# Earlier and later places for pieces of a hand-written schedule: spectral mixing, then routed experts, on one core

## The chip, the cores and the metric

One core of one Trainium2 chip runs the whole kernel in one launch. The metric is device time in microseconds: the median of three timed runs. A profile is one further execution under the hardware profiler, with a time of its own.

## What is computed

```python
X = np.fft.rfft(x, axis=1)                 # x: (8, 2496, 256), fp32
F = (filt_r + 1j * filt_i)[None, :, :]
y = np.fft.irfft(X * F, n=x.shape[1], axis=1)
x = y.reshape(19968, 256)
expert_idx = token_ids * 2654435761 % 8
for e in range(8):
    mask = expert_idx == e
    h = np.maximum(x[mask] @ w1[e], 0.0)   # w1: (8, 256, 1024)
    out[mask] = h @ w2[e]                  # w2: (8, 1024, 256)
```

A sequence of 2496 = 39 x 64 rows is transformed, filtered and transformed back; then every row goes through the one of eight two-layer networks that its token number picks.

## The kernel before, in words

**Mixing.** Each of the eight batches goes through three stages. Stage 1 takes the products of length 39 (`stage1`, six units, products `pa`, recorded at L267 and L261 with their copies on ScalarE); its result is written to a DRAM tile `d1` (L297) and read back in another layout (`load2`, L303). Stage 2 has ten blocks: `forward` (products `pb`, L312, and four VectorE operations: y at L318, two z at L322, the sum at L323) and `back` (products `pc`, L335, whose copies go through the DRAM tile `d2`). Stage 3 (`load4` reads at L406, `stage3` makes the products `pd`, again L267 and L261) puts rows into tiles `o`, and GpSimd scatters each of them (L433, an indirect DMA) into the array `xs`, at a place that belongs to the row's expert. In the first two batches parts are done on the chip in another form: `turn2` (transposes `pt`, L367), `back_c` (products `pc`, L378, copied at L380) and `turn4` (transposes `pu`, L394).

**Experts.** `xs` is cut into 85 tiles of 256 rows, ordered in five stages so that the tiles of a stage need the first 2, 3, 4, 6 or all 8 batches. Step i works on tile i: `up` (eight groups of products in banks a, b, c, L886, with sums of weights that GpSimd prepares at L876, a copy of bank a on ScalarE at L897, VectorE additions at L893 and relus on ScalarE at L890) and `down` (L921). The rows of a tile are asked for by `load`: four DMA issues of `xg` and one of `no` (L843), from tile 2 on out of ScalarE's queue. `ask(i)` loads tile i+2, if it has not been loaded; inside `down`, `spot` asks one tile further ahead when that tile belongs to the same stage. So the requests of an ordinary tile go out in `down`, and those of tile 2 and of the first tile of each later stage in `up`, at `ask(i)`.

**The order.** A manual schedule: what is written first stands first on its engine's queue. The list `head` holds pairs of a due number and a piece; the numbers only sort. Everything in `head` stands ahead of step 0: the table loads, the routing (`count`, `route`, `tile_experts`, `experts` on VectorE, `later` and `places` on GpSimd), the first two batches whole, stage 1 of the third and most of the fourth. `chain(k)` at 22+3k issues `turn2(k+1)`, `back_c(k-2)` and `forward(k)` of the first batch. The list `main` holds what is mixed into the steps: `part1`, `part2` and `part3` give stage 1, 2 and 3 of a batch numbers in steps, `within` squeezes them, and `run_until(t)` issues all with a number below t at fixed points: i+.6 ahead of `down`, i+.7, .8 and .9 inside it, i+1 after it.

**Buffers.** The products of all mixing stages share four PSUM buffers (`fps`); `y` and `z` share three SBUF buffers (`ppool`); the input tiles `x` of a batch share two (`xpool`). A piece that takes a buffer waits for the last reader of the piece that held it.

`warm(n)` multiplies the identity by itself n times into bank a; nobody reads the result.

Of the kernel before, what the change touches and what calls it, by code (L numbers as in the profile page):

```python
# [36 lines left out]
NU = (HN + XG) // XG  # L37
# [88 lines left out]
def kernel(  # L126
# [314 lines left out]
    first, second = batches[:2]  # L441
# [255 lines left out]
    def pads(k):  # L697
        blank = ppool.tile([P, 2 * C], I32, name=f"blank_{k}", tag="p")[:, 0:W]
        nc.vector.memset(blank[:, 0:C], 0)
        nc.vector.memset(blank[:, C:], N)  # L700
        for q in (2 * k, 2 * k + 1):
            scatter(blank.bitcast(F32), at_i[:, q:q + 1], "xs_pad")
# [19 lines left out]
    def spaced(t0, t1, n):  # L722
        return [t0 + (t1 - t0) * u / n for u in range(n)]

    def within(todo, share=.5):

        return [(t // 1 + .5 + t % 1 * share, piece) for t, piece in todo if t is not None]

    def part1(b, at, loads):
        bt = batches[b]  # L730
        return within([(at[u], lambda u=u: bt.stage1(u)) for u in range(NU)] +
                      [(loads[v], lambda v=v: bt.load1(v)) for v in range(NV)])

    def part2(b, at, loads, lag):
        bt = batches[b]
        return (within([(at[u], lambda u=u: bt.forward(u)) for u in range(NS // 2)], .3) +
                within([(at[u] + lag, lambda u=u: bt.back(u)) for u in range(NS // 2)] +
                       [(loads[g], lambda g=g: bt.load2(g)) for g in range(NS // SG)]))

    def part3(b, at, loads):  # L740
        bt = batches[b]
        return within([(at[u], lambda u=u: bt.stage3(u)) for u in range(NU)] +
                      [(loads[v], lambda v=v: bt.load4(v)) for v in range(NV)])
# [6 lines left out]
    def chain(k):  # L750

        for step, j in ((Batch.turn2, k + 1), (Batch.back_c, k - 2), (Batch.forward, k)):
            if 0 <= j < N_2:
                step(first, j)

    def warm(n):

        ps = banks["a"].tile([P, 4, P], F32, name="warm", tag="a")
        for k in range(n):
            nc.tensor.matmul(out=ps[:, k % 4, :], lhsT=ident[:], rhs=ident[:], start=True, stop=True)  # L760

    third = batches[2]
    head = [(0, lambda: warm(14))]
# [7 lines left out]
    head += [(t, lambda k=k: way_back(k)) for k, t in enumerate((21.91, 31.2))]  # L771
    head += [(21.95, lambda: first.turn2(0))]
    head += [(22 + 3 * k, lambda k=k: chain(k)) for k in range(N_2 + 2)]
    head += [(t, lambda u=u: second.stage1(u)) for u, t in enumerate((28.5, 31.5, 37.5, 40.5, 46.5, 47))]
    head += [(50 + .1 * g, lambda g=g: second.load2(g)) for g in range(4)]
    head += [(67, lambda: second.load2(4))]
    head += [(t, lambda u=u: first.room(u)) for u, t in enumerate((50, 53.5, 56.5, 61, 75.5, 80))]
    at = (56, 57.8, 63, 69, 75, 79.5)
# [5 lines left out]
    head += [(t, lambda k=k: weights(k // 2, k % 2)) for k, t in enumerate((90, 90.1, 90.2, 90.3))]  # L784
    head += [(90.2 + 4.6 * u - 1.5 * (u > 0), lambda u=u: [second.turn4(u), second.room(u)]) for u in range(NU)]
    head += [(91.8 + 4.6 * u, lambda u=u: second.stage3(u)) for u in range(NU)]
    head += [(93.3 + 4.6 * u + 4 * (u > 3), lambda u=u: third.stage1(u)) for u in range(NU)]
    head += [(100, blanks)]
    fourth = batches[3]
    head += [(t, lambda v=v: fourth.load1(v)) for v, t in enumerate((110.5, 110.6))]  # L790
    head += [(123.5, lambda: begin()), (123.6, lambda: [load(i) for i in range(2)])]
    head += [(124, lambda: [nc.sync.dma_start(out=dram, in_=chip) for dram, chip in put_off[2]])]
    head += [(125 + .1 * g, lambda g=g: third.load2(g)) for g in range(4)]
    head += [(126, lambda: [nc.sync.dma_start(out=dram, in_=chip) for dram, chip in put_off[3]])]
    head += [(123 + .1 * u, lambda u=u: fourth.stage1(u)) for u in range(4)]
    todo = [(t - 200, piece) for t, piece in head]
    todo += [(t, lambda k=k: pads(k)) for k, t in enumerate((10.9, 11.6, 11.9, 16.9, 17.6, 17.95, 22.9))]

# [8 lines left out]
        return out  # L807

    todo += part2(2, spaced(1, 3.5, N_2), [None] * 4 + [1.5], .6)
    todo += part3(2, spaced(4.6, 7.5, NU), [4.0, 4.1, 4.8]) + part1(3, [None] * 4 + [1.5, 2], [None, None, .5])  # L810
    todo += part2(3, spaced(6.4, 10, N_2), [5.2, 5.4, 5.6, 6.5, 7.5], .6)
    todo += part3(3, spaced(12, 16, NU), [11.2, 11.4, 12.5])
    todo += batch(4, (7.5, 11), (12.4, 16.4), (18.3, 22.3)) + batch(5, (13, 17), (18.4, 21.6), (23.2, 26.8))
# [1 line left out]
    for e in range(E):  # L815
        t = 34.3 + 1.5 * e
# [10 lines left out]
    def begin():  # L827
        nonlocal gath, work, outs, nums, tpool
        rctx.close()
        tpool, nums, gath = [pool(ctx, f"tp{k}", 1) for k in range(2)], pool(ctx, "nums", 8), pool(ctx, "gath", 2)  # L830
        outs, work = pool(ctx, "outs", 2), pool(ctx, "work", 1)
        weight_sums(0, nc.vector)

    def load(i):

        g = gath.tile([P, TB // 32, C // 4], F32, name=f"xg_{i}", tag="xg")
        no = nums.tile([P, 2], I32, name=f"no_{i}", tag="no")
        rows = xs[tiles[i] * TB:(tiles[i] + 1) * TB, :]
        moves = [(g[32 * q:32 * q + 32, :, :], rows[:, 64 * q:64 * q + 64].rearrange("(a t) c -> t a c", t=32))
                 for q in range(4)]  # L840
        moves.append((no[:].bitcast(F32), rows[:, C:C + 1].rearrange("(h p) c -> p (h c)", p=P)))
        for k, (to, src) in enumerate(moves):
            ld = (nc.sync if i < 2 and (i or k < 3) else nc.scalar).dma_start(out=to, in_=src)  # L843
            for b in range(STAGES[stage_of[i]], B):
                tc.declare_no_dep(ld.ins, group=f"xs_{b}", reason="the tiles of a stage hold tokens of its batches alone")
            if stage_of[i] < G - 1:
                tc.declare_no_dep(ld.ins, group="xs_pad", reason="places without a token lie in the last stage alone")
            tc.add_to_no_dep_group("xs_read", ld.ins)
        xg[i], to_rows[i] = g, no
# [26 lines left out]
            eng.tensor_tensor(t[k][:], p, q, op=OP.subtract)  # L876
        sums[i] = t

    def up(i, ht, between=lambda: None):
        w1, x, st, t = ws[i][0], parts[i], parts[i]["sums"], sums[i]  # L880
        ps = {k: banks[k].tile([P, 4, P], F32, name=f"up_{i}_{k}", tag=k) for k in "abc"}
        h11, h12, h21, h22 = [ht[:, h, 4 * f:4 * f + 4, :] for h in range(2) for f in range(2)]

        def product(bank, w, xx, first, fs=range(4)):
            for f in fs:
                nc.tensor.matmul(out=ps[bank][:, f, :], lhsT=w[:, f * P:(f + 1) * P], rhs=xx,  # L886
                                 start=first and f == 0, stop=True, skip_group_check=True)

        def relu(out, in_):
            nc.scalar.activation(out=out, in_=in_, func=AF.Relu)  # L890

        def plus(out, bank, other):
            nc.vector.tensor_tensor(out, ps[bank][:], other, op=OP.add)  # L893

        h = F // 2
        product("a", w1[:, 0, 0:h], x[0, 0], True)
        nc.scalar.copy(out=h21, in_=ps["a"][:])  # L897
        between()
        product("b", t[1], st[:, 1, :], True)
        plus(h12, "b", h21)  # L900
        product("c", t[0], st[:, 0, :], True)
        plus(h22, "c", h21)
        product("a", w1[:, 1, 0:h], x[0, 1], False, (0, 1))
        product("b", t[2], st[:, 2, :], False)
        plus(h22, "b", h22)
        relu(h22, h22)
        product("a", w1[:, 1, 0:h], x[0, 1], False, (2, 3))
        relu(h11, ps["a"][:])
        product("c", w1[:, 1, h:], st[:, 3, :], False)
        plus(h12, "c", h12)  # L910
        relu(h12, h12)
        product("b", t[3], x[1, 1], False)
        plus(h21, "b", h21)
        relu(h21, h21)
# [112 lines left out]
    def ask(i, sooner=False):  # L1027

        j = asked[0]
        if j <= i + 2 or (sooner and j == i + 3 < NT and stage_of[j] == stage_of[j - 1]):  # L1030
            if j < NT:
                load(j)
                asked[0] += 1
# [7 lines left out]
    def run_until(t):  # L1041
        while main and main[0][0] < t:
            main.pop(0)[1]()

    def late_step(i):
        ht = work.tile([P, 2, FP, P], F32, name=f"ht_{i}", tag="ht")
        store(i - 1, (1,))
        if i + 1 < NSURE:
            weight_sums(i + 1)
        store(i - 1, (0,))  # L1050
        both(i, ht)

    def step(i):
        if i >= WS:
            late_step(i)
            return
        ht = work.tile([P, 2, FP, P], F32, name=f"ht_{i}", tag="ht")
        if i + 1 < NSURE:
            weight_sums(i + 1)
        if i > 0:  # L1060
            store(i - 1)
        up(i, ht, lambda: ask(i))
        weights(i + 2, 0)
        if i + 1 < NSURE:
            token_parts(i + 1)
            token_sums(i + 1)
        run_until(i + .6)
        down(i, ht, lambda k: spot(i, k))
        weights(i + 2, 1)
        run_until(i + 1)  # L1070
# [59 lines left out]
```

## Time and profile before

| | us |
|---|---|
| median of 3 timed runs | 1466.7 (1465.14 to 1467.44) |
| the profiled execution: time, span | 1423.94, 1422.2 |
| mean granted TensorE clock in it | 0.991 |
| TensorE busy | 1372.1 |
| first up product (step 0 begins) | 141.38 |
| first scatter of the second batch | 106.50 |

How to read the profile: a line of the timeline has the start, the busy time, the engine, the line of the code, the operation, its output and inputs, and in brackets the idle time of that engine before it and what ended that. PE is TensorE, DVE VectorE, ACT ScalarE, POOL GpSimd, SP SyncE; a q behind the engine's name (ACTq, SPq) means its queue issuing a DMA. A line of the stretches has, for each engine, busy time and instructions, and at the end the granted TensorE clock as a share of full speed, the DMA engines' busy share and the GB/s that they moved.

### The profile page before, as it was taken

The numbers are of one execution on the slowest core, as the hardware profiler recorded it, in microseconds if no ns is written. First come the engines' busy times: TensorE is split into PE (matmuls) and PEld (weight loads), VectorE is DVE, ScalarE is ACT, GpSimd is POOL, SyncE is SP. The second block draws the span as 40 slices with busy tenths as digits, with TensorE's granted clock in tenths as the row PEclk, the third lists the DMA queues.
The fourth block names the chain that finished last, engine by engine and source line by source line (L and its number), as shares of the span: only waits on it lengthen the run. The fifth ranks groups of instructions, "written<-read, shape, count | busy, mean of one in ns | idle before, by whom it ended". The sixth has DMA issues, their size and how long they took to land.

```text
span 1422.2 us, 26307 instructions
## 1 busy us (share of the span) xinstructions
PE 1372.1 (96%) x9398; PEld 1272.3 (89%) x9398; DVE 888.2 (62%) x1630; ACT 417.2 (29%) x760; POOL 828.3 (58%) x735
## 2 busy tenths in 40 slices
PE   8988999999999999999999999999999999999997
PEld 7776888988888988889999899999999999999997
DVE  7673475575556566445766377656767776777775
ACT  4544122223232223232223222222222222222222
POOL 6157143844665565578533587788845566555563
PEclk9999899999999999999999999999999999999999
DMA  8786765858987698888754775887742526161611
GB/s 230 204 275 172 223 206 121 274 187 246 272 259 223 182 289 268 251 265 272 242 167 128 221 256 173 231 242 236 253 139 67 192 57 203 46 217 40 219 46 35
DMA packets 244650, 278.34 MB, mean 196 GB/s; under 512 B 125171, under 2 KB 213862, under 8 KB 235092
## 3 DMA queue, kind: packets, MB, share of 16 engines
q1 hardware_dynamic: 98020, 182.34, 40.7%
q10 hardware_dynamic: 126688, 50.07, 14.4%
q0 software_dynamic: 19808, 44.20, 8.8%
q8 instruction: 77, 1.26, 0.4%
q14 instruction: 57, 0.47, 0.1%
HBM read 293.65 MB, written 86.15 MB: 267 GB/s over the span
## 4 chain that ended last, share of the span: by engine, by line
PE 85%; DMA 7%; DVE 5%; issue 1%; ACT 1%; SPq 1%; ACTq 0%; POOL 0%; POOLq 0%; DVEq 0%
PE dps L921 20%; PE up_b L886 9%; PE up_a L886 6%; PE up_c L886 5%; PE pd L267 5%; PE pb L312 4%; PE dnc L948 4%; PE dnb L948 4%; PE upc L943 4%; PE dna L948 4%; PE upa L943 4%; PE pa L267 4%; PE pc L335 3%; PE upe L943 2%; PE upb L943 2%; PE upg L943 2%
## 5 line engine op out<-in xcount | busy, mean ns | idle before, releaser
L921 PE MATMUL dps<-wts,ht 128*128 128x256 f32 x1600 | 370.2, 382 | 4.9 <-ACT ht L890 4.9
L921 PEld LDWEIGHTS dps<-wts,ht 128*128 128x128 f32 x1600 | 304.3, 191 | 49.1 <-ACT ht L890 6.1
L1013 POOL DMA_INDIRECT out_dram<-osb,no x158 | 165.2, 1045 | 223.5 <-DVE osb L955 137.2
L433 POOL DMA_INDIRECT xs<-o,sidx x176 | 177.7, 1009 | 169.6 <-ACT o L269 94.0
L876 POOL TENSOR_TENSOR tw<-wts 128x512 f32<-128x512 f32 x158 | 204.3, 1293 | 110.9 <-DMA wts<-in_moe_w_dram 98.8
L876 POOL TENSOR_TENSOR tw<-wts,tw 128x512 f32<-128x512 f32 x158 | 206.1, 1304 | 6.2
L893 DVE TENSOR_TENSOR ht<-up_b,ht 128x512 f32<-128x512 f32 x150 | 103.7, 691 | 117.9 <-PE up_b L886 91.1
L890 ACT ACTIVATE ht<-ht 128x512 f32<-128x512 f32 x150 | 94.3, 630 | 189.0 <-DVE ht L893 169.0
L322 DVE TENSOR_TENSOR z<-pb,filt 64x512 f32<-64x512 f32 x160 | 110.2, 689 | 30.0 <-PE pc L335 28.0
L926 DVE COPY osb<-dps 128x512 f32<-128x512 f32 x50 | 34.5, 691 | 148.1 <-PE dps L921 147.8
L886 PE MATMUL up_a<-xt,wts 128*128 128x128 f32 x800 | 115.5, 277 | 11.0 <-ACT ht L897 6.3
L886 PEld LDWEIGHTS up_a<-xt,wts 128*128 128x128 f32 x800 | 105.9, 193 | 14.8 <-ACT ht L897 7.1
L886 PE MATMUL up_b<-st,tw 128*128 128x128 f32 x800 | 107.5, 278 | 3.6 <-DVE ht L893 2.2
L886 PEld LDWEIGHTS up_b<-st,tw 128*128 128x128 f32 x800 | 98.1, 193 | 5.7 <-issue 5.1
L893 DVE TENSOR_TENSOR ht<-up_c,ht 128x512 f32<-128x512 f32 x100 | 69.0, 690 | 38.0 <-PE up_c L886 33.2
L952 ACT ACTIVATE ht<-ht 128x512 f32<-128x512 f32 x90 | 56.6, 630 | 121.5 <-DVE ht L955 72.7
L267 PE MATMUL pd<-t,wi_t 120*117 120x256 f32 x320 | 77.5, 385 | 3.1 <-DMA t<-d 2.2
L318 DVE TENSOR_TENSOR y<-pb,filt 128x512 f32<-128x512 f32 x80 | 55.1, 689 | 40.5 <-PE pb L312 38.2
L323 DVE TENSOR_TENSOR y<-y,z 128x512 f32<-128x512 f32 x80 | 74.4, 930 | 2.7
L269 ACT COPY o<-pd 117x512 f32<-117x512 f32 x80 | 44.9, 585 | 101.6 <-PE pd L267 51.6
L897 ACT COPY ht<-up_a 128x512 f32<-128x512 f32 x50 | 29.4, 587 | 150.2 <-PE up_a L886 109.2
L312 PE MATMUL pb<-low,d_t 128*128 128x256 f32 x280 | 72.3, 381 | 0.6 <-DVE z L322 0.6
(215 smaller groups left out, 2422.5 us busy)
## 6 DMA issues: line engine op xcount, KB each, us to landing
wts<-in_moe_w_dram SPq DMA_DIRECT2D x162, 1024.0 KB
xg<-xs ACTq DMA_DIRECT2D x321, 64.0 KB
low<-d SPq DMA_DIRECT2D x70, 256.0 KB
d_t<-t2s SPq DMA_DIRECT2D x15, 1024.0 KB
e_t<-t2s SPq DMA_DIRECT2D x15, 1024.0 KB
x<-in_x_dram SPq DMA_DIRECT2D x39, 312.0 KB
t<-d SPq DMA_DIRECT2D x12, 960.0 KB
raw<-in_moe_w_dram SPq DMA_DIRECT2D x8, 1024.0 KB
```

The lines of the kernel that those rows point to most:

```text
L267: nc.tensor.matmul(out=ps[0:cols * H, k, :], lhsT=w[:], rhs=src[:, 2 * i + k, :], start=True, stop=True)
L312: nc.tensor.matmul(out=ps[:, i, :], lhsT=d_t[:, s, :], rhs=rhs, start=True, stop=True)
L322: nc.vector.tensor_tensor(out=z[b], in0=ps[a], in1=f_t[1][64 * hi:64 * hi + 64, s1:s1 + 2, :], op=OP.mult)
L433: st = nc.gpsimd.indirect_dma_start(out=xs[:], out_offset=bass.IndirectOffsetOnAxis(ap=index, axis=0), in_=rows, in_offset=None, bounds_ch ...
L876: eng.tensor_tensor(t[k][:], p, q, op=OP.subtract)
L886: nc.tensor.matmul(out=ps[bank][:, f, :], lhsT=w[:, f * P:(f + 1) * P], rhs=xx, start=first and f == 0, stop=True, skip_group_check=True)
L890: nc.scalar.activation(out=out, in_=in_, func=AF.Relu)
L893: nc.vector.tensor_tensor(out, ps[bank][:], other, op=OP.add)
L921: nc.tensor.matmul(out=ps[:, h, :], lhsT=ht[:, h, fp, :], rhs=w2[:, fp, :], start=(fp == 0), stop=(fp == FP - 1))
L943: nc.tensor.matmul(out=ps[:, f, :], lhsT=w[:, f * P:(f + 1) * P], rhs=xx, start=first and f == 0, stop=True, skip_group_check=True)
L948: nc.tensor.matmul(out=ps[:, 0, :], lhsT=a[:, f, :], rhs=b[:, f, :], start=first and f == 0, stop=True, skip_group_check=True)
L1013: st = nc.gpsimd.indirect_dma_start(out=out[:], out_offset=bass.IndirectOffsetOnAxis(ap=to_rows[i][:, h:h + 1], axis=0), in_=o[:, h, :], i ...
```

## The change

- Stage 1 of the second batch: units 0 and 1 one place of the chain later, units 4 and 5 after the forward products of block 9, around the back products of block 8. Its reads (`load2`) are numbered behind the last unit.
- Stage 1 of the third batch: units 0 and 1 ahead of the last two back products of the second batch's stage 2, units 2 and 3 where 0 and 1 were, units 4 and 5 at the end as before.
- The first two loads of the fourth batch's input are numbered 95 and 99.5 instead of 110.5 and 110.6.
- 14 idle products (`warm`) behind the fourth batch's stage 1, ahead of step 0.
- Stage 3 of the third batch about half an issuing point later. By the fixed points: unit 0 goes from inside `down` of step 4 to behind it, units 1 to 4 one point on, unit 5 stays.
- `ask(i)` goes from behind the copy of bank a to behind the whole of `up`, so behind the relus on ScalarE's queue. The late steps (from 50 on, `both`) are not changed.

```diff
-    head += [(t, lambda u=u: second.stage1(u)) for u, t in enumerate((28.5, 31.5, 37.5, 40.5, 46.5, 47))]
-    head += [(50 + .1 * g, lambda g=g: second.load2(g)) for g in range(4)]
+    head += [(t, lambda u=u: second.stage1(u)) for u, t in enumerate((31.5, 34.5, 37.5, 40.5, 49.5, 52.5))]
+    head += [(53 + .1 * g, lambda g=g: second.load2(g)) for g in range(4)]
...
-    head += [(93.3 + 4.6 * u + 4 * (u > 3), lambda u=u: third.stage1(u)) for u in range(NU)]
+    head += [(t, lambda u=u: third.stage1(u)) for u, t in enumerate((87, 89.9, 93.3, 97.9, 114.9, 115))]
...
-    head += [(t, lambda v=v: fourth.load1(v)) for v, t in enumerate((110.5, 110.6))]
+    head += [(t, lambda v=v: fourth.load1(v)) for v, t in enumerate((95, 99.5))]
...
+    head += [(123.55, lambda: warm(14))]
...
-    todo += part3(2, spaced(4.6, 7.5, NU), [4.0, 4.1, 4.8]) + part1(3, [None] * 4 + [1.5, 2], [None, None, .5])
+    todo += part3(2, spaced(4.85, 7.6, NU), [4.0, 4.1, 4.8]) + part1(3, [None] * 4 + [1.5, 2], [None, None, .5])
...
-    def up(i, ht, between=lambda: None):
+    def up(i, ht):
...
         product("a", w1[:, 0, 0:h], x[0, 0], True)
         nc.scalar.copy(out=h21, in_=ps["a"][:])
-        between()
         product("b", t[1], st[:, 1, :], True)
...
-        up(i, ht, lambda: ask(i))
+        up(i, ht)
+        ask(i)
         weights(i + 2, 0)
```

## The prediction

> **What bounds the kernel now.** I read the page's busy shares first, then the chain of waits, then TensorE's timeline for its gaps, and from each gap the timeline of the engine it waits for.
>
> ```profile
> PE 1372.1 (96%) x9398; PEld 1272.3 (89%) x9398; DVE 888.2 (62%) x1630; ACT 417.2 (29%) x760; POOL 828.3 (58%) x735
> PE 85%; DMA 7%; DVE 5%; issue 1%; ACT 1%; SPq 1%; ACTq 0%; POOL 0%; POOLq 0%; DVEq 0%
> ```
>
> TensorE is the bound: 96% busy, 85% of the chain. No matmul is removed, so only its gaps and its clock can change. Those that the edits touch:
>
> ```profile
> 29.64 1.96 PE L267 MATMUL pa<-wts,wf_t 117*120 117x256 f32 x8 [1.18 <-DMA wts<-in_x_dram]
> 32.87 1.13 PE L378 MATMUL pc<-e_t,y 128*128 128x128 f32 x8 [0.69 <-DVE z L322]
> 60.62 1.62 PE L378 MATMUL pc<-e_t,y 128*128 128x128 f32 x8 [2.11 <-DVE o L412]
> 69.04 1.03 PE L312 MATMUL pb<-low,d_t 128*128 128x256 f32 x4
> 141.38 2.08 PE L886 MATMUL up_a<-xt,wts 128*128 128x128 f32 x8 [4.66 <-DVE xt L854]
> 152.56 8.86 PE L921 MATMUL dps<-wts,ht 128*128 128x256 f32 x32 [2.27 <-ACT ht L890]
> 240.44 1.99 PE L267 MATMUL pd<-t,wi_t 120*117 120x256 f32 x8 [2.20 <-DMA t<-d]
> 501.64 3.54 PE L921 MATMUL dps<-wts,ht 128*128 128x256 f32 x8 [2.61 <-ACT ht L890]
> ```
>
> Columns: start, busy time, operation, the gap before it and who ended it. The first down products of step 0 (152.56) and of step 18 (501.64) wait for relus on ScalarE, whose timeline says why:
>
> ```profile
> 143.71 5.49 ACTq L843 DMA_DIRECT2D xg<-xs  x4
> 150.93 0.41 ACTq L843 DMA_DIRECT2D no<-xs  x1
> 151.39 0.63 ACT L890 ACTIVATE ht<-ht 128x512 f32<-128x512 f32 x1 [7.31 <-DMA xg<-xs]
> 494.37 4.51 ACTq L843 DMA_DIRECT2D xg<-xs  x4
> 500.47 0.63 ACT L890 ACTIVATE ht<-ht 128x512 f32<-128x512 f32 x1 [6.12 <-DVE xt L854]
> ```
>
> Issuing a tile's row requests held ScalarE 7.6 us (143.71 to 151.34) and 6.1 us, with the relus behind. The clock by stretch (one before the last figures):
>
> ```profile
> 33.00:38.00 5.00, 5.00 (x33) 4.62 (x34) 4.82 (x9) 2.84 (x5) 4.40 (x6) 1.00 0.96 282
> 140.00:147.00 7.00, 5.62 (x29) 5.62 (x30) 3.31 (x7) 0.59 (x1) 2.17 (x2) 0.54 0.84 192
> 498.00:505.00 7.00, 4.39 (x18) 3.54 (x17) 3.87 (x7) 2.15 (x4) 5.41 (x5) 0.76 1.06 292
> ```
>
> The clock fell to half after the gaps of 4.66, 2.61 and 2.27 us, not after 2.20. Lastly the queues that matter:
>
> ```profile
> 33.77 1.50 DVE L664 TENSOR_TENSOR past<-rt,last 128x40 f32<-128x40 f32 x1
> 36.78 1.39 DVE L322 TENSOR_TENSOR z<-pb,filt 64x512 f32<-64x512 f32 x2
> 60.35 13.44 SPq L303 DMA_DIRECT2D low<-d  x10
> 106.50 0.98 POOL L433 DMA_INDIRECT xs<-o,sidx  x1 [9.26 <-ACT o L269]
> 134.74 0.89 POOL L433 DMA_INDIRECT xs<-o,sidx  x1 [0.30 <-issue]
> ```
>
> **What the Trainium skill says.** "TensorE: Matmul & The Clock Gate", Part 1: the clock is halved after an idle window of about 3.4 us, returns after a busy one, and the windows run freely. The trace agrees in kind: gaps from 2.3 us up can halve it, for 3.0 to 6 us. "DMA: Bandwidth & Descriptors", Two DMAs through the same engine are not ordered: a DMA that reads what another wrote must wait for that one's semaphore. So the second batch's rows go out and back in full: last write issued at 56.7, reads at 60.35. "Perfetto Trace Analysis", Tensor Engine Instruction: ScalarE, VectorE and GpSimd are strict FIFO, as the relus behind the requests show.
>
> **Part by part**, against the profiled execution of 1423.94 us (span 1422.2 and 1.7 around it). The median of the timed runs is 42.8 us higher; I carry the difference over unscaled.
>
> *Second batch's stage 1 later.* The unit stood at 29.64 (1.73 us of TensorE by the pitch of its neighbours, two ScalarE copies; SP's writes follow the copies). Without it pc 1 needs y 1 alone (28.54+2.05=30.59) and starts at 30.74, pb 3 at 31.6, pe at 32.9, done 33.5. Then comes the moved unit, and in the changed program its PSUM buffer is the one that pb 3 held: it waits for z 3. VectorE reaches z 3 behind the tile_experts chain (L664 at 33.77 to L670 at 36.06) and ends it at 38.17. So TensorE stands idle from 33.5 to 38.3, 4.8 us, where it was wholly busy. After 4.66 us the clock fell; I expect it here too, some 4.2 us at half speed, 2.1 us lost. Counting on at the pitches of this stretch (pa 1.73, pt .58, pc .89, pb .87, VectorE 2.85 a block): pa 38.3 to 41.8, pb 4 at 43.5 (38.35 before), pb 7 at 56.0 (49.40), pc 7 at 60.1 behind y 7, the last unit behind z 9 at 65.1 (54.34 before), pc 9 at 66.1 (60.62). The tail gaps are filled, and the cold stretch before (61.5 to 67.5) goes: pu at 68.0 (63.02), then 3.85 to pb of the second batch, 71.9. But its rows start from that last unit: before, from 54.34 to the first reads 6.0 us; the DMA share shows 0.5 MB in by about 63.1, with 0.6 to be seen 63.7, so 9.35 in all. 65.1+9.35=74.5 against 69.04: **+5.5**. Bounds: clock kept 72.45, +3.4; stall and cold stretch twice as long, +8. The 2.6 us wait at 71.9 may halve the clock again, 1.5 if so: +0.7 (0 to 1.5).
>
> *Third batch's stage 1 earlier.* Its first two units fill the gaps before the last two back products (1.25 and 1.72 us before). Units 2 and 3 take the places that these had between 104 and 125, so 3.46 us of TensorE leave that stretch; two waits on VectorE's copies (0.5 each) come there and one goes. The copies on ScalarE and one write issue (0.36) stand ahead of pc 9's copy, +0.1. None of this sets block 0: GpSimd's 22 scatters do, 1.29 us each without a pause from 106.50 to 135.63, then 5.75 to the first up product (141.38). Their start moves with the first pd. **-0.3** (hiccups of 0.61 and 0.43 in that row: -1.3 to +0.3). The fourth batch's six loads move up on SP behind the weights, wait for the freed x tiles, and have only block 0's requests behind them, 20 us later: 0; if that cover goes, those requests wait.
>
> *Idle products.* 14 at 0.223 us (4 of up_a take 0.89) are 3.1 us. Block 0's slow clock costs 2.5 (up part 8.74 against 6.25 us). But stage 1 now ends 2.6 us earlier relative to block 0 (3.46-0.5-0.1-0.3), so after the products 4.66+2.6-3.1, some 4.1 us, are still idle, enough to halve the clock again, only later: **-0.6** (0 to -2.5).
>
> *Row requests behind the relus.* Only step 0 and the first tiles of a later stage (steps 8, 18, 28, 48) issue there; the others' requests come in the down part. Step 0: the wait (2.44 by the starts) and the cold excess (8.69-6.91=1.78): **-4.2**. Step 18: 2.61+(3.54-1.89): **-4.3**. Queued behind the requests now: the next step's copy of up_a, and pc and pd copies. Two tiles' requests stand together, 7.6+4.4 us at worst: +0.4 for each of the two (0 to 4), +0.2 for the other steps.
>
> *Third batch's stage 3 later.* pd at 240.44 waits for t till 240.4. It now comes behind eight more down products (1.73), so the wait falls from 2.2 to 0.5: **-1.7** (-2.2 to 0). Its copies and scatters come with it; the last unit keeps its place, so stage 1's tiles are not later.
>
> Sum: 5.5+0.7-0.3-0.6-4.2-4.3+0.8+0.2-1.7 = **-3.9**; 1423.9 to 1420.0, and 1466.7 to 1462.8.
>
> **The rivals.**
> *The early wait is cheap.* If z 3 comes sooner or the clock holds and the second batch's rows come in time, the shift is 1 instead of 6.2, and the sum -9.1: 1457.6. For it: TensorE has slack to give back in the tail. Against: VectorE's order puts tile_experts ahead of z 3 whatever TensorE does.
> *Back to nothing.* The clock falls at the early wait, at 72 and again in block 0 with two windows each: shift 9 instead of 6.2, no gain from idle products: -0.5, 1466.2. Against: the gaps of 2.20 us at 240.44 and 2.10 at 396.92 left the clock whole.
> *ScalarE held later (slower).* One mechanism: with two tiles' requests in a row, step 1's up_a copy comes 5 us late, TensorE stalls 3.4 and runs cold 1.8; at step 18 the pd copies are late likewise, 3.6. The holds h cost 8.8 where I count 0.8: +4.1, 1470.8. It decides from h = 4.7. For it: the requests at 381.87 held ScalarE 13 us, and a copy behind them cost 2.10 us at 396.92. Against: the copy has 4 to 5 us more to spare than the relus.
>
> **How the numbers follow.** Forecast 0.40, cheap wait 0.25, back to nothing 0.20, ScalarE held 0.15. A change under 0.2% (2.9 us) can't be told from none. Faster: most of the forecast and the cheap wait, 0.57; same: the rest of the forecast and nearly all of the third, 0.28; slower 0.15. The range 1456.0 to 1469.5 takes in the cheap wait to -10.7 and the held ScalarE up to +2.8.
>
> **What would show it.** Right: a gap of about 4.8 us before pa near 38, ended by z L322, and half clock after it; pb of the second batch waiting for DMA near 72; no gap before the first down products of steps 0 and 18; block 0 still cold; a short wait before the first pd of batch 2. Wrong: TensorE dense from 34 to 57; the first scatter of batch 1 at or before 106.5; gaps before up_a in step 1.

## The result, and the profile after

| | median us | runs |
|---|---|---|
| before | 1467.07 (1463.31 to 1470.06) | 6 |
| after | 1480.31 (1476.92 to 1491.57) | 6 |

The changed kernel takes 1.0103 of the time before, 95% interval 1.0064 to 1.0143: slower by 1.0%, about 13 us, where 3.9 us less was forecast.

The kernel before takes 1425 us on one chip (e0 to e3; the profile of before has that time too) and 1463 to 1467 us on others (the timed runs, the profile after, and all later experiments; "the 1464 us chips" below). So the spans 1422.2 and 1475.2 of the two pages do not stand for the change; ratios below are always within one chip, and step lengths are compared between profiles of the same time level.

One more thing on reading the lines of DMA issues (SPq, ACTq): a line with x4 puts four issues together, and its second number runs from the start of the first to the end of the last, with the pauses between them. It is not busy time, as the note ahead of the prediction has it.

The page after, busy line and chain:

```profile
PE 1398.1 (95%) x9426; PEld 1289.0 (87%) x9426; DVE 865.6 (59%) x1630; ACT 415.6 (28%) x760; POOL 825.8 (56%) x735
PE 83%; DMA 7%; DVE 5%; issue 2%; ACT 1%; another core or an unknown queue 1%; SPq 0%; ACTq 0%; POOLq 0%; POOL 0%; DVEq 0%
```

TensorE is still the bound. Its timeline after, at the places that the prediction showed of before:

```profile
30.33 1.25 PE L378 MATMUL pc<-e_t,y 128*128 128x128 f32 x8 [3.27 <-DVE y L323]
...
39.79 1.96 PE L267 MATMUL pa<-wts,wf_t 117*120 117x256 f32 x8 [3.15 <-issue]
...
59.95 1.13 PE L378 MATMUL pc<-e_t,y 128*128 128x128 f32 x8 [0.72 <-DVE y L323]
...
75.23 1.65 PE L312 MATMUL pb<-low,d_t 128*128 128x256 f32 x4 [2.98 <-DMA low<-d]
...
170.99 1.85 PE L887 MATMUL up_a<-xt,wts 128*128 128x128 f32 x8 [2.29 <-DVE xt L855]
...
178.95 7.07 PE L921 MATMUL dps<-wts,ht 128*128 128x256 f32 x32
...
264.46 1.99 PE L267 MATMUL pd<-t,wi_t 120*117 120x256 f32 x8 [0.29 <-DMA t<-d]
```

Most of the signs that the prediction asked for are there: a wait before the moved unit (39.79), the second batch's rows late (75.23; 74.5 was said), block 0 still at a slow clock (1.85 for eight products, 1.05 in step 1), no gap before the down products of steps 0 (178.95) and 18, a short wait before the third batch's stage 3. One is missing: the moved unit waits 3.15 us, not 4.8, and then runs at full clock (1.96; 1.89 is its time elsewhere). A large loss stands elsewhere, at two places that the prediction had put down with 0.2 us. Again TensorE after, in steps 8 and 29:

```profile
345.16 1.10 PE L312 MATMUL pb<-low,d_t 128*128 128x256 f32 x4 [0.51 <-issue]
...
350.42 1.10 PE L312 MATMUL pb<-low,d_t 128*128 128x256 f32 x4 [1.58 <-DVE z L322]
...
749.90 0.71 PE L887 MATMUL up_a<-xt,wts 128*128 128x128 f32 x4 [3.28 <-ACT ht L898]
750.72 1.35 PE L887 MATMUL up_b<-st,tw 128*128 128x128 f32 x8
```

In the last two the second product of bank a waits 3.28 us for ScalarE's copy, and the clock falls behind it (1.35 for what takes 1.06).

### The profile page after: what moved, and what is told of

It reads as the page before. It is cut to its first block, busy times and chain, and to the rows that moved or that the text cites. A ratio compares the mean times of both kernels' runs of the same rounds, so it can differ in the third digit from the quotient of the medians.

```text
span 1475.2 us, 26362 instructions
## 1 busy us (share of the span) xinstructions
PE 1398.1 (95%) x9426; PEld 1289.0 (87%) x9426; DVE 865.6 (59%) x1630; ACT 415.6 (28%) x760; POOL 825.8 (56%) x735
## 4 chain that ended last, share of the span: by engine, by line
PE 83%; DMA 7%; DVE 5%; issue 2%; ACT 1%; another core or an unknown queue 1%; SPq 0%; ACTq 0%; POOLq 0%; POOL 0%; DVEq 0%
PE dps L921 19%; PE up_b L887 9%; PE up_c L887 5%; PE up_a L887 5%; PE pd L267 5%; PE pb L312 4%; PE pa L267 4%; PE dnc L948 4%; PE dnb L948 4%; PE dna L948 4%; PE upc L943 4%; PE upa L943 4%; PE pc L335 3%; DMA t<-d 2%; PE upe L943 2%
## 5 line engine op out<-in xcount | busy, mean ns | idle before, releaser
L921 PEld LDWEIGHTS dps<-wts,ht 128*128 128x128 f32 x1600 | 302.1, 190 | 44.4 <-issue 1.8
L894 DVE TENSOR_TENSOR ht<-up_b,ht 128x512 f32<-128x512 f32 x150 | 103.6, 691 | 141.4 <-PE up_b L887 79.4
L267 PEld LDWEIGHTS pd<-t,wi_t 120*117 120x117 f32 x320 | 58.0, 186 | 23.1 <-issue 6.3
```

The costliest lines, as they stand in the source:

```text
L267: nc.tensor.matmul(out=ps[0:cols * H, k, :], lhsT=w[:], rhs=src[:, 2 * i + k, :], start=True, stop=True)
L921: nc.tensor.matmul(out=ps[:, h, :], lhsT=ht[:, h, fp, :], rhs=w2[:, fp, :], start=(fp == 0), stop=(fp == FP - 1))
```

## Experiments

Edits are against the kernel before unless another is named; times are medians, and "us" behind a ratio is the ratio's distance from 1 times the median of before on that chip.

**The parts one by one** (four runs on the 1425 us chip).

```diff
 # e0: nothing
 # e1: requests only
-        up(i, ht, lambda: ask(i))
+        up(i, ht)
+        ask(i)
 # e2: second batch only
-    ... second.stage1(u)) for u, t in enumerate((28.5, 31.5, 37.5, 40.5, 46.5, 47))]
-    head += [(50 + .1 * g, lambda g=g: second.load2(g)) for g in range(4)]
+    ... second.stage1(u)) for u, t in enumerate((31.5, 34.5, 37.5, 40.5, 49.5, 52.5))]
+    head += [(53 + .1 * g, lambda g=g: second.load2(g)) for g in range(4)]
 # e3: third batch's stage 1 and the fourth's loads only
-    head += [(93.3 + 4.6 * u + 4 * (u > 3), lambda u=u: third.stage1(u)) for u in range(NU)]
+    head += [(t, lambda u=u: third.stage1(u)) for u, t in enumerate((87, 89.9, 93.3, 97.9, 114.9, 115))]
-    ... fourth.load1(v)) for v, t in enumerate((110.5, 110.6))]
+    ... fourth.load1(v)) for v, t in enumerate((95, 99.5))]
```

> The kernel before, unchanged. Its profiled execution was 43 us below its own timed median, the changed kernel's was not; so the two profiles may differ by more than the change. If that execution was an exception, this profile has a span near 1465 us and shows waits that the first one lacks, in the prelude too (first up product later than 141). If not, span near 1424 again. Time 1467.

Measured: 1425.38 us, ratio 0.9993 (0.9977 to 1.0010). Two copies of one kernel agree within 0.2%.

> The kernel before with one part of the change: a tile's row requests behind the relus. My prediction: steps 0 and 18 start their down products without a wait, -7.5 us, 1459. The rival in which ScalarE is held later: +5 to +13 us, 1472 to 1480, with waits for the copy of bank a in steps 1, 9, 19, 29.

Measured: 1432.64 us, 1.0051 (1.0034 to 1.0069), +7.3 us. Missed by some 15 us, and inside the rival's range: the part that was to bring most is the one that costs most. Of the waits for bank a that the rival named, those in steps 1 (2.13 us) and 29 (3.45 us) are there, those in steps 9 and 19 are not; step 8 is longer by another wait.

> The kernel before with stage 1 of the second batch at its later places alone. Theory A (the loss sits here: pa waits for z 3, then half clock, then the second batch's rows come late): +6 to +12 us, 1473 to 1479. Theory B (the loss comes from the third batch's stage 1, whose copies stand ahead of others on ScalarE): within 3 us of before.

Measured: 1432.91 us, 1.0046 (1.0026 to 1.0065), +6.6 us. Right, and by the mechanism: in e2's timeline of TensorE the moved unit waits 4.76 us (4.8 was said), runs at half clock (3.74 for what takes 1.89), and the second batch's first product waits for its rows. The trace names nobody for the first wait ("issue"), but z 3 on VectorE ended at 38.53, 0.10 us ahead of the unit, as in the profile after (39.69 and 39.79):

```profile
38.63 3.74 PE L267 MATMUL pa<-wts,wf_t 117*120 117x256 f32 x8 [4.76 <-issue]
...
76.91 1.10 PE L312 MATMUL pb<-low,d_t 128*128 128x256 f32 x4 [3.08 <-DMA low<-d]
```

> The kernel before with stage 1 of the third batch in the tail gaps of the second batch's stage 2 and the fourth batch's two loads earlier, alone. Theory A and my prediction: -1 to +1 us, since GpSimd's scatters set the start of step 0. Theory B: +6 to +13 us, 1473 to 1480, with waits before the third batch's pa and the second batch's pd products.

Measured: 1421.21 us, 0.9975 (0.9952 to 0.9999), -3.6 us; expected was next to nothing. TensorE ahead of the second batch's stage 3, in e0:

```profile
103.29 1.92 PE L378 MATMUL pc<-e_t,y 128*128 128x128 f32 x8 [1.72 <-DVE y L323]
105.99 1.96 PE L394 MATMUL pu<-ident,high 128*120 128x128 f32 x8 [0.78 <-ACT high L380]
107.98 3.09 PE L267 MATMUL pd<-t,wi_t 120*117 120x256 f32 x8
```

and in e3:

```profile
101.12 1.89 PE L267 MATMUL pa<-x,wf_t 117*120 117x256 f32 x8
102.85 1.06 PE L378 MATMUL pc<-e_t,y 128*128 128x128 f32 x8
104.81 1.09 PE L394 MATMUL pu<-ident,high 128*120 128x128 f32 x8 [0.91 <-ACT high L380]
106.34 1.99 PE L267 MATMUL pd<-t,wi_t 120*117 120x256 f32 x8 [0.44 <-DVE t L398]
```

In e0 the clock fell to half behind three gaps (1.25, 1.72 and 0.78 us): pc, pu and pd take 1.92, 1.96 and 3.09 us. In the profile of before the same three gaps had left it whole:

```profile
100.97 1.13 PE L378 MATMUL pc<-e_t,y 128*128 128x128 f32 x8 [1.72 <-DVE y L323]
102.88 1.09 PE L394 MATMUL pu<-ident,high 128*120 128x128 f32 x8 [0.78 <-ACT high L380]
104.41 1.99 PE L267 MATMUL pd<-t,wi_t 120*117 120x256 f32 x8 [0.44 <-DVE t L398]
```

That profile is the exception. Of the eleven profiles with the third batch at its old place the other ten have this pd at 2.8 to 3.8 us; in all nine with the part moved it takes 1.98 or 1.99. The scatters follow the first pd: first one at 108.38 instead of 111.00, last at 135.69 instead of 139.39, and step 0 begins at 142.36 instead of 146.01. On the 1464 us chips step 0 begins between 155.1 and 168.6 with either place, so how the gain gets to the end is shown on the 1425 us chip alone. The edit also moves the fourth batch's two loads, and no run separates the two; the traces put no wait of TensorE between 60 us and step 0 down to input rows.

**The other two parts, and two ways to mend the requests** (four runs on a 1463.6 us chip).

```diff
 # e4: idle products only
+    head += [(123.55, lambda: warm(14))]
 # e5: stage 3 of the third batch later only
-    todo += part3(2, spaced(4.6, 7.5, NU), ...
+    todo += part3(2, spaced(4.85, 7.6, NU), ...
 # n1: as e1, and one tile a step (last[0] is the step of the last request)
-        if j <= i + 2 or (sooner and j == i + 3 < NT and ...):
+        if j <= i + 2 or (sooner and last[0] < i and j == i + 3 < NT and ...):
 # n2: ask(i) stays at its old place, its request is issued by SP (steps below 50)
+                load(j, not sooner and i < WS)
-            ld = (nc.sync if i < 2 and (i or k < 3) else nc.scalar).dma_start(out=to, in_=src)
+            ld = (nc.sync if sp or i < 2 and (i or k < 3) else nc.scalar).dma_start(out=to, in_=src)
```

> The fourteen idle products ahead of block 0 alone. The prediction's own term: the wait for step 0's tokens goes on some 4 us after them, so the clock halves again and nothing is gained but 0.6 us: 1424.5 us. Rival, the products keep the clock up: in the run of before on this chip the first three products of step 0 took 2.08, 1.92 and 1.84 us against 1.05 in step 1, so at most 2.7 us: 1422.4. Rival, they run late and stand before the first product: up to 1.5 us slower, 1426.6.

Measured: 1461.33 us, 0.9999 (0.9972 to 1.0025). As the prediction had it: after the idle products (3.29 us) TensorE still waits 5.33 us, and step 0's first products take 2.04, 1.91 and 1.90 us, as slow as before.

> The third batch's stage 3 a quarter step later, alone. The prediction's own term: its first product waits 1.7 us for its rows in the run of before on this chip (before pd in step 4), and that wait goes: 1423.4 us. Rival, the wait only moves to another product or the later stage 3 presses the steps behind it: 1425.1 or above.

Measured: 1465.13 us, 1.0003 (0.9984 to 1.0023). No difference that can be told from noise. The wait for the rows falls to 0.4 us in its profile, and step 5 is 1.0 us longer (17.6 against 16.6).

> Requests behind the relus as in the change, but a step that has asked for one tile does not ask for the next one as well; that is asked for in the step after. The theory (the two tiles' ten requests, 10 us of ScalarE, start 10 us later than before in step 0 and 9 us later in step 28, and so reach the copy of bank a in the step after, which was 3.2 and 4.6 us late): the gain of step 0 (4.2 us) and of step 18 (2.5) stays, the losses of steps 1 (4.8), 8 (2.6) and 29 (6.5) go: about 1419 us, 1416 to 1422. Rival, it is not the second tile: any request behind the relus reaches the next copy: 1430 or above. Rival, rows asked for a step later come too late for their step: above 1432.6.

Measured: 1487.96 us, 1.0181 (1.0146 to 1.0217), +26.5 us. A miss, and the rival of late rows is not it: VectorE waits for no tile's rows after the first, as in e5. Two things can be read from it. In step 29 no product of bank a waits for its copy, so that wait needs the second tile's requests in step 28; step 8 is 24.4 us long all the same, so its loss does not. The further losses (steps 4, 12 to 14, 19, 20, and another wait of 1.9 us in 29) come with every later request at a new place; they were not followed up.

> The request that stands between copy and relus in before stays at its place in the program, but SP issues it at the five steps where it happens. The theory (it is ScalarE's time that counts, and not the transfer): the wait of the first down products goes in step 0 (4.2 us with the clock) and in step 18 (2.5), nothing is held in steps 1 and 29: about 1418.5 us, 1416 to 1422. Rival, SP's own transfers behind it come late by the 2 to 5 us of the issue, and stage 2 of the third batch waits for them: 1425 or above.

Measured: 1469.84 us, 1.0048 (1.0020 to 1.0075), +7.0 us. A miss that shows what a request costs its engine. SP and ScalarE (its DMA queue and its copy) in n2, step 1:

```profile
173.60 8.28 SPq L843 DMA_DIRECT2D xg<-xs  x4
...
173.67 10.05 ACTq L843 DMA_DIRECT2D xg<-xs  x4
...
183.76 0.47 ACTq L843 DMA_DIRECT2D no<-xs  x1
...
184.32 0.59 ACT L897 COPY ht<-up_a 128x512 f32<-128x512 f32 x1 [15.81 <-DMA xg<-xs]
```

SP reached the first tile's request only behind its own transfers, at the very time at which ScalarE issued the second's. ScalarE's four issues take 0.31 to 0.76 us each; in the pauses between them it waits until transfers of SP have landed. The trace's chain of waits for step 1 (start, length, what) has the last of them:

```profile
173.00 10.38 DMA d<-high
...
183.41 0.31 ACTq L843
```

SP had issued that write at 173.00; only when it had landed, 10.38 us later, did ScalarE issue its fourth request. So the theory that ScalarE's time counts and not the transfer fails here. The copy of bank a in step 1, whose product had ended at 174.92, came at 184.32; TensorE waited 8.25 us for it. In step 19 a copy of bank a comes late again and TensorE waits 7.57 us.

**The whole change with parts taken out** (four runs on a 1465 us chip; f1 has the second batch's lines of before, f2 the request's place of before, f3 both).

> The whole change, beside three kernels that each leave a part of it out. First theory: the parts add up, +7.3 us (requests), +6.6 (second batch), -3.6 (third batch), 0 (idle products and stage 3 later): 1.007 of before. Rival: the parts hide or feed each other, and the whole is the 1.010 measured first, or less than the second batch's part alone (1.0045).

Measured: 1473.13 us, 1.0053 (1.0033 to 1.0073), +7.8 us, near the sum of the parts that was said (1.007) and below the 1.010 measured first.

> The change with the second batch's stage 1 and its rows back at their old times. First theory (its wait for bank f's fourth buffer and the late rows cost 6.6 us of themselves): 0.0046 less than the whole change, about 1.0025. Rival (in the whole change another wait stands in its place, or the requests' loss grows when block 0 starts earlier): within 0.002 of the whole change.

Measured: 1468.69 us, 1.0032 (1.0012 to 1.0053), +4.7 us; less is gained by leaving the part out than was said (0.0021 instead of 0.0046).

> The change with the requests back between copy and relus. First theory (the request for a second tile, pushed into the next step, costs what e1 showed): 0.005 less than the whole change, about 1.002. Rival (where block 0 starts later and before has no wait ahead of its first down products, as in the profiles of e4 and e5, the order of the requests is worth nothing either way): within 0.002 of the whole change.

Measured: 1464.90 us, 0.9999 (0.9975 to 1.0024), -0.1 us: 0.0054 below the whole change, as said.

> Only the third batch's stage 1 and the fourth's loads earlier, the idle products and stage 3 of the third batch later. First theory: these keep the 3.6 us of e3: 0.9975 of before, faster than both kernels. Rival (the gain was the clock's alone, and block 0 begins when GpSimd's 22 scatters are done): 1.000 within 0.002.

Measured: 1462.84 us, 0.9983 (0.9963 to 1.0003), -2.5 us; between the theory (0.9975) and the rival (1.000 within 0.002), and settled by neither.

By difference the requests cost 7.9 us (f0 and f2) or 7.2 (f1 and f3), as on the other chip; the second batch's part 3.1 (f0 and f1) or 2.3 (f2 and f3), half of e2's; the rest brings 2.5. They add up to within 1 us.

The lengths of the steps, from first up product to first up product, say where the requests cost it. Left pair: the 1425 us chip; right pair: the 1464 us chips, before's place (e4, e5, f2, f3) and behind the relus (after, f0, f1).

| step | e0 | e1 | before's place | behind the relus |
|---|---|---|---|---|
| 0 | 20.0 | 15.8 | 15.5 to 16.1 | 14.9 to 16.0 |
| 1 | 20.5 | 25.3 | 22.0 to 25.7 | 21.0 to 21.6 |
| 8 | 21.8 | 24.4 | 21.8 to 22.3 | 24.4 in all |
| 18 and 19 | 41.8 | 40.2 | 44.4 to 49.4 | 44.8 to 48.5 |
| 29 | 20.1 | 26.6 | 20.1 to 20.2 | 25.6 to 26.5 |

Step 0's 4.2 us come back in step 1 in e1, and in the four profiles of the 1464 us chips they aren't there to be gained; step 1 is shorter there behind the relus, but g1's median (below) shows nothing of that. Steps 18 and 19 together gain 1.5 at most; steps 8 and 29 lose 2.1 to 2.6 and 5.4 to 6.5 us in each of these profiles. ScalarE around step 28 (which begins at 686.84 in e0 and at 689.91 in e1), in e0:

```profile
688.22 1.95 ACTq L843 DMA_DIRECT2D xg<-xs  x4
...
694.63 1.82 ACTq L843 DMA_DIRECT2D xg<-xs  x4
...
698.47 0.59 ACT L338 COPY low<-pc 128x512 f32<-128x512 f32 x1 [3.83 <-PE pc L335]
699.48 1.68 ACTq L342 DMA_DIRECT2D d<-low  x2
702.81 0.59 ACT L897 COPY ht<-up_a 128x512 f32<-128x512 f32 x1 [3.76 <-DMA d<-low]
```

and in e1:

```profile
697.33 1.82 ACTq L843 DMA_DIRECT2D xg<-xs  x4
...
700.83 4.87 ACTq L843 DMA_DIRECT2D xg<-xs  x4
...
706.31 0.59 ACT L338 COPY low<-pc 128x512 f32<-128x512 f32 x1 [8.59 <-DMA xg<-xs]
709.20 1.22 ACTq L342 DMA_DIRECT2D d<-low  x2
710.46 0.59 ACT L897 COPY ht<-up_a 128x512 f32<-128x512 f32 x1 [3.56 <-issue]
```

Counted from the start of the step, the first tile's requests come 6.0 us later in e1 and the second's 3.1 us (the "9 us" in n1's expectation holds the 3 us by which all of e1 runs later). SP loads three input tiles in the same window. What its queue waits for at these loads, first in e0, then in e1 (total, times, longest):

```profile
SPq L249 <- DMA wts<-in_moe_w_dram: 3.4, 1, 3.4
```

```profile
SPq L249 <- DMA xg<-xs: 6.9, 1, 6.9
```

and the chain of waits in e1:

```profile
697.33 7.32 DMA xg<-xs
...
704.66 4.46 DMA x<-in_x_dram
...
709.20 0.46 ACTq L342
...
709.69 0.72 ACTq L342
...
710.46 0.59 ACT ht L897
...
711.09 1.01 PE up_a L886 x3
```

A transfer in this chain counts from its issue to its landing. The third input load waits until the first tile's rows have landed (7.32 us); ScalarE's writes of stage 2 wait until that load has landed (4.46 us); and behind the writes stands step 29's copy of bank a, whose product ended at 705.85. It starts at 710.46, 4.6 us late; TensorE waits 3.45 us and runs below full clock until about 717. The rows, the load and the writes share no data: in the trace each of them waits on the semaphore that the one before it sets when it lands. With the requests at their new place the same load waits for another transfer (in e0 for weights). The second tile's issues stretch from 1.82 to 4.87 us in the same way: each takes 0.31 to 0.46 us, and the second of them waits for an input load of SP to land. It is not enough that SP is at work beside them: the second tile's in e0 (694.63) and the first tile's in e1 (697.33) also stand between SP's loads, and take 1.82 us. The profile after has the same chain (rows 7.62 us, load 4.09), and so has f0 (7.56 and 4.52); in g2 and f1 the rows' landing (7.08 and 7.53 us) holds the second tile's own requests, and behind them a copy of stage 2, the writes and the copy of bank a.

In step 8 another wait is at work. A product pb waits until VectorE's z of the pb before it is done (1.58 us, the line at 350.42 of the profile after), in each of the six profiles with the request at its new place there and in no other; in e0 the same pb starts before that z. What makes it wait for that z was not followed.

**The place of the loss, and what is left of the rest** (four runs on a 1463.6 us chip).

```diff
 # g1: (0, 18); g2: (8, 28); g4: as f3, and (0, 18)
-        up(i, ht, lambda: ask(i))
+        behind = i in (0, 18)
+        up(i, ht, lambda: behind or ask(i))
+        if behind:
+            ask(i)
 # g3: of e2 only the last two units and the rows
-    ... second.stage1(u)) for u, t in enumerate((28.5, 31.5, 37.5, 40.5, 46.5, 47))]
+    ... second.stage1(u)) for u, t in enumerate((28.5, 31.5, 37.5, 40.5, 49.5, 52.5))]
```

> Requests behind the relus at steps 0 and 18 alone, the three other stage starts as in before. Theory (the loss sits at steps 8 and 28, where the second tile's request is pushed into another queue's transfers; at 18 the wait of the down products goes, 2 to 4 us, less 1 in step 19; at step 0 there is nothing to gain where before has no wait there): 0.998 to 1.000 of before. Rival (the loss is in step 1, next to step 0's second request): 1.003 or above.

Measured: 1463.47 us, 1.0002 (0.9984 to 1.0020). The rival (1.003 or above) is out; a gain of the size that was said for step 18 isn't to be seen.

> Requests behind the relus at steps 8 and 28 alone. Theory: stage 2's product pb waits in step 8 (2.6 us longer) and the second product of bank a in step 29 (6.4 us longer), 9 us in all: 1.006 of before, and both waits at the same places in the trace. Rival (the waits there have another cause, a chance of where the transfers stand): 1.000 within 0.002.

Measured: 1473.24 us, 1.0074 (1.0050 to 1.0098), +10.8 us. With g1 this settles the place: the loss goes where the edit at steps 8 and 28 goes. TensorE in g2, the same three waits as in the profile after:

```profile
333.27 1.10 PE L312 MATMUL pb<-low,d_t 128*128 128x256 f32 x4 [0.51 <-issue]
...
338.54 1.10 PE L312 MATMUL pb<-low,d_t 128*128 128x256 f32 x4 [1.57 <-DVE z L322]
...
742.83 0.71 PE L886 MATMUL up_a<-xt,wts 128*128 128x128 f32 x4 [3.00 <-ACT ht L897]
```

> Of the second batch's part only the last two units of stage 1 and its rows later; its first two units stay at their old times. Theory of the prediction (the first unit, one place later, takes the buffer behind pb 3 and waits for z 3: that wait and half the later start are gone; the rows still come late, a wait of about 3 us ahead of pb near 74): half the part's cost at most, 1.001 to 1.002. Rival (all of the cost comes from the late rows): the same as the whole part, which was 1.0046 on one chip and 1.0016 to 1.0021, by difference, on another.

Measured: 1462.25 us, 0.9992 (0.9972 to 1.0012). Its product pb of the second batch waits 3.00 us for its rows, until 69.48; the kernels with this part as before begin it between 67.2 and 72.7 us on these chips, those with the whole part at 75.2 to 76.8. So the second batch's cost comes with its first two units, whose wait pushes all that follows; the later last units and rows alone cost nothing that can be told.

> The parts that lost nothing together: third batch's stage 1 and fourth's loads earlier, idle products, stage 3 of the third batch later, requests behind the relus at steps 0 and 18 alone. Theory: 0.9983 (without requests) less the 1 to 3 us of step 18: 0.9970, faster than both kernels. Rival: step 18's gain is given back at once by the transfer it pushes: 0.9983 or above.

Measured: 1461.05 us, 0.9983 (0.9966 to 1.0001). The rival holds: steps 0 and 18 add nothing to f3.

**A faster version** (two runs on a 1463.9 us chip: h2 is e3's edit, h1 that and g3's).

> The third batch's part (stage 1 and the fourth's loads earlier) with the last two units of the second batch's stage 1 and its rows later, nothing else. Theory: 0.998 from the third batch and 0.999 from the second's last units add: 0.9975, faster than both kernels. Rival (both fill the same gaps ahead of the second batch's stage 3): 0.9985 or above.

Measured: 1461.74 us, 0.9984 (0.9962 to 1.0006). Nearer to the rival: the last units add nothing to h2.

> The third batch's part alone, again: it gave 0.9975 on one chip with an interval that all but touches 1, and 0.9983 together with idle products and stage 3 later. Theory (two products fill the gaps ahead of the second batch's stage 3, its first product starts some 2 us earlier and at full clock): 0.9975 to 0.9985. Rival (chance of that chip): 1.000.

Measured: 1462.34 us, 0.9982 (0.9958 to 1.0006). Where the theory had it, though its interval takes in 1.

Five kernels hold the third batch's part without a part that costs (e3, f3, g4, h1, h2): 0.9975 to 0.9984, all below 1, four with an interval that just passes it. The third batch's part alone is the version to take, 2.6 to 3.6 us faster than before in its two runs (h2 and e3); the other parts add nothing that can be measured.

## Why the prediction was wrong

- **Row requests behind the relus: -4.2, -4.3, +0.4, +0.4, +0.2, together -7.5; measured +7.2 to +7.9.** This is the step that failed, and with it the sign. Two errors. The larger is the term "+0.2 for the other steps": steps 8 and 28 cost 9 us by the step lengths and 10.8 in g2. I had priced a hold at its new place by the spare time of one copy. I did not ask what an issue on the queue waits for, nor what waits for its landing: at the new place the rows land 7.3 us after their issue, SP's load starts behind that, and ScalarE's writes behind the load. In step 8 it is a wait for a z. The other error is the two gains: both were read from one profile, and 4.2 and 4.3 us there are not in the median (g1: 1.0002), because the hold comes and goes (of the eight profiles on the 1464 us chips with step 0's request at its old place only g2, g3 and h1 have a wait before the down products, of 2.3, 1.4 and 1.5 us) and because the step behind takes back what is left.
- **"Issuing a tile's row requests held ScalarE."** The hold is there, but not all of it is issuing: of the 6.1 us at step 18 some 4 are waits for landings, of the 7.6 us at step 0 1.7. The chain of waits in the profile of before, at step 18:

```profile
488.24 11.78 DMA low<-d
...
500.04 0.38 ACTq L843
...
500.47 1.12 ACT ht L890 x2
...
501.64 1.65 PE dps L921 x3
```

  SP had issued this read at 488.24; ScalarE's last request, and with it the relus, had to wait until it had landed at 500.02. Such a hold changes with every transfer that moves.
- **The rival "ScalarE held later".** Right in its result: a copy of bank a 4.6 us late, a stall of 3.45 and a cold stretch (5, 3.4 and 1.8 us were said), though through landings on both queues and not through the requests' own time. Its place was step 1, where e1 shows it (2.13 us of waiting, 4.8 in all) and of the five profiles on the 1464 us chips with step 0's request behind the relus only g4 does (1.44 us); it missed steps 8 and 29. I gave it 0.15 because "the copy has 4 to 5 us more to spare than the relus"; the chain used that up.
- **Second batch's stage 1: +5.5 and +0.7.** Right on the 1425 us chip (+6.6 in e2, the stall to the tenth), half as much on the 1464 us chips (+2.3 to +3.1 by difference). In the profiles after and f0 the moved unit waits 3.15 and 2.56 us and keeps its clock, in f2 3.70 us and it does not. What takes the rest back there is not shown: f2's profile is still 4.1 us behind f3's at step 2.
- **Third batch's stage 1: -0.3.** Measured -3.6 and -2.6. The argument "none of this sets block 0: GpSimd's 22 scatters do" holds on the 1425 us chip, but the scatters start with the first pd, and ahead of that one the clock falls in ten of eleven profiles; I had read the eleventh. A term that was mis-sized by a clock that held in one execution. Nor does the clock need a gap of 2.3 us to fall, as I had it: e0 shows three shorter ones, and in the profile of before it stood at half from 61.5 to 67.5 us, behind the gap of 2.11 us that the prediction shows at 60.62.
- **Idle products: -0.6.** 0.9999 and a clock still halved: as said, within the interval.
- **Third batch's stage 3 later: -1.7.** 1.0003, interval -2.3 to +3.4 us; the wait goes as said, and step 5 gives back 1.0.
- **The range** reached to 2.8 us above before, since it took in the held ScalarE at two steps only and set against it gains that the median does not have; the whole change lies 7.8 (f0) to 13 us above.

The Trainium skill, "Perfetto Trace Analysis", DMA Instruction — HWDGE (DVE, Sync), says that the block which generates descriptors is locked by the queue that uses it, and that the recorded time of an issue contains the wait for that lock. Where the loss arises the traces show no such wait: the second tile's requests in e1 are recorded with 0.31 to 0.46 us each, and the time goes by between them. Long records do occur (SP's first request in n2, 4.77 us), but also without the other queue: in e0 four requests stretch over 5.89 us from 453.44 on, with records of up to 2.2 us, while SP issues nothing between 448.5 and 463.9. Whether the lock has a part in these is not shown. "DMA: Bandwidth & Descriptors", Issuing engines are not separate DMA queues, calls the sequencer's time to initiate a DMA usually small relative to the DMA itself. The traces agree: 0.31 to 0.46 us to issue a request of 64 KB, 7.32 us until the rows have landed (e1); it is the waiting for landings that costs.

What stays open: the difference between 1.0103 and 1.0053 for the same kernel in two sets of runs (their intervals overlap), the wait in step 8, the further losses of n1, and what returns half of the second batch's cost.

## What to carry to other kernels

Before a DMA issue is moved on an engine that also computes, list what the other issuing queues do in the new window and which later issues of the same queue move along; look up in the trace which landing each of these issues waits for, and what waits for its own; then follow the first compute instruction behind all of them to its reader. A gain read from one stall counts only if the stall is in more than one execution, and if the next step does not hold its twin. Small gaps on TensorE that add up are worth filling even where another engine sets the date: behind such gaps the clock fell in ten of eleven profiles here.

## What the runs showed of the hardware

- A row request of 64 KB takes ScalarE's queue 0.31 to 0.46 us to issue (e1, from 700.83 on), and its rows land 7.32 us after the issue (e1, 697.33). The four of a tile stretch from 1.82 us up to 4.87 us there when an issue between them waits for a landing, and to 10.05 us in n2.
- Transfers of the two queues hold each other up through their landings, without sharing data: SP's input load waits 6.9 us for ScalarE's rows (e1), ScalarE's request 10.38 us from the issue of SP's write (n2) and 11.78 us from that of SP's read (before).
- Three gaps of 1.25, 1.72 and 0.78 us within 7 us went ahead of a clock at half in one execution (0.50 of full speed from 104 to 110 us in e0) and left it whole in another (1.00 in the profile of before) of the same kernel.
- The kernel before has two levels, 1425 us (one chip) and 1464 us (two others). In the profiles of e4, e5, g1 and g2 block 0 begins at 155.6 to 168.6 us instead of 141.4 and 146.0 (before and e0), and step 6 takes 26 us instead of 18.3. What makes the levels is not shown.
